# Eight batches of linear attention into a two-layer network: the third batch's first product as one plain product instead of seven

## The chip, the cores and the metric

The kernel runs on one core of a Trainium2 chip. The metric is the device time of one execution in microseconds. A core has TensorE (PE; its weight loads are listed as PEld), VectorE (DVE), ScalarE (ACT), GpSimd (POOL) and the queue of SyncE (SP), from which nearly all transfers are issued. Each engine works through its own instructions in the order in which they were written and waits by semaphores for the others, so a waiting instruction holds up everything behind it on its engine.

## The reference

There are 8 batches of 8 heads, 576 positions and 64 numbers per head. From q and k come feature vectors of 128 numbers, from those and v the attention output, and this output (4608 rows of 512) goes through two matrices with a leaky ReLU between them:

```python
r = np.maximum(x, 0.0); phi = np.concatenate([r * cos_w, r * sin_w], axis=-1)   # for q and k
kv  = np.einsum('bhsf,bhsd->bhfd', phi_k, v); z = np.sum(phi_k, axis=2)
out = np.einsum('bhsf,bhfd->bhsd', phi_q, kv) / (np.einsum('bhsf,bhf->bhs', phi_q, z)[..., None] + 1e-06)
x   = out.transpose(0, 2, 1, 3).reshape(4608, 512)
h   = x @ w_in                      # (4608, 512) @ (512, 2048)
y   = np.maximum(0.01 * h, h) @ w_out   # (4608, 2048) @ (2048, 512)
```

## The kernel before

The rows are cut into nine groups of 512: groups 0 to 7 are the first 512 positions of each batch, group 8 the last 64 positions of all eight. For each group the kernel makes the attention output (sum over k and v: `kv_sum`, L314; product with q and division: `num` and `divide`, L403 and L421, the result in the tile `xs`), turns it round so that features lie on partitions (tile `xT`), makes the first product (x by w_in) with the leaky ReLU into the tile `g`, and then the second product (`g` by w_out).

Both products exist in two forms. The plain form of the first product (`ffn1`, L475) takes 16 units for a group; a unit, called M, is four matmuls of 512 columns, and after every second unit ACT applies the leaky ReLU to 1024 columns. The form by seven (`ffn1s`, L619) is Strassen's: 4 parts of 7 products, each product a unit of four matmuls of 256 columns, 28 units in all. It needs sums of weight blocks (`w1_sum`, L579, eight operations once, kept in the tile `wext`), sums of blocks of xT (`x_sum`, L595, four for each group) and, for each of its parts, three copies, two additions and four leaky ReLUs of 512 columns (`ffn1e`, L649) on ACT and DVE. It works in four PSUM banks `ps_f`, which take the place of the two double banks `ps_h` of the plain form once that is no longer used. The second product by seven (`ffn2s`, L729) has 28 units too, called F here, F0 to F27, of four matmuls of 256 columns; it needs sums of `g` (`g_sum`, L681) and, once, of w_out (`weight_sum`, L540). Group 0 is plain in both products. `G7 = 1` and `F7 = 2` say from which group on the second and the first product go by seven: the first product is plain for groups 0 and 1.

The order of everything after the first groups is written out. Stretch g of the program interleaves the second product of group g with the first product of group g+1; a string for each stretch (`O`) gives the order of the units: F is a unit of the second product, M a plain one of the first, a digit a product of the seven, other letters the operations behind them. All other work has a place, a number on the same axis (16 places for each stretch; stretch 1 runs from 16 to 32), and `weave` (L915) puts it into the program in front of the unit that follows its place. A letter in the strings `e`, `We`, `Xe` names the engine for it: D is DVE, A ACT, P POOL. For batch b these are the loads (`L`), the feature maps of q (`q_prep`, two operations for each of four row blocks) and of k (`k_cos`, `k_sin`, nine each), the copies of v (`v_pairs`, two), the transposes of q's features by DMA, `kv_sum`, four `num`, and the transposition of `xs` to `xT`. The tiles for k's features (`kp`), for v (`vm`) and for `xs` exist once, so the next batch's may be written only after the last reader of the one before.

For groups 3 to 8 `xT` comes from a DMA transpose issued on SP. For group 2 it comes from TensorE (`x_transpose`, L382): for each of four row blocks four small transposes into the PSUM tile `ps_x` and a copy by ACT. That tile covers two banks; row blocks 0 and 1 lie in the first, 2 and 3 in the second. A write of TensorE into a bank waits for the copy out of that bank.

k, v and q arrive in four staging buffers (`stage`); some go to the tiles `ext` and `wext` instead, before these are needed for sums (`stage_tile`, L104).

Of the kernel before, what the change touches and what calls it, by code (L numbers as in the profile page):

```python
# [9 lines left out]
dt = mybir.dt  # L10
# [10 lines left out]
def kernel(  # L21
# [15 lines left out]
    B, H, S, D = q.shape  # L37
# [10 lines left out]
    NKC = DM // P  # L48
# [1 line left out]
    NG = B + 1  # L50
    NE = D + 2
    G7 = 1
    F7 = 2

    ctx.enter_context(tc.manual_schedule())

# [31 lines left out]
    def need(*keys):  # L88
        for key in keys:
            assert key in done, key  # L90
# [58 lines left out]
    w1 = {}  # L149
# [95 lines left out]
    kv = [const.tile([P, H, NE], dt.float16, name=f"kv{b}") for b in range(B)]  # L245
# [136 lines left out]
    def x_transpose(g, j, eng):  # L382

        need(("num", g, j))
        if j == 0:
            st["ps_x", g] = psum("h", [P, J, NKC, P], dt.float16, "ps_x")
        ps = st["ps_x", g][:, j]
        for c in range(NKC):
            nc.tensor.transpose(ps[:, c], st["xs", g][:, j, 2 * c : 2 * c + 2, :], ident)  # L389
        copy(eng, xT_tile(g)[:, j], ps)  # L390
        if j == J - 1:
            done.add(("xT", g))
# [430 lines left out]
    held = []  # L823
# [185 lines left out]
    for m in range(6):  # L1009
# [4 lines left out]
    units = []  # L1014

    TUNE = {'B': {2: {'L': None,
               'e': 'DDDDDPADAAAAPDPPPPPDDDAA',
               'kc': [14.1499, 14.4499, 14.3249, 14.3749, 13.9249, 14.4249, 13.8499, 14.2999, 14.2499],
               'ks': [14.3499, 14.0999, 14.0749, 14.2749, 14.1749, 14.2249, 14.1249, 13.7749, 14.3999],
               'mm': 16.0956,  # L1020
               'n': [16.4042, 17.139, 17.6138, 18.1982],
               'q': [10.357, 10.4856, 10.5499, 10.8713],
               'qT': [10.7428, 12.6999],
               'v': [13.3499, 10.9356],
               'x': [17.3129, 17.6764, 18.8869, 18.939],
               'xe': 'AAAA'},
           3: {'L': [10.6142, 13.1999, 13.4249, 18.1356],
               'e': 'AADADAAAPAPAAPAPDDAPADPA',
               'kc': [18.9042, 17.1651, 19.0521, 18.8347, 18.7042, 16.6173, 17.8347, 18.2295, 17.526],
               'ks': [19.3529, 17.4477, 17.4869, 19.226, 16.8173, 17.6451, 17.1912, 19.0129, 17.7077],  # L1030
               'mm': 20.4434,
               'n': [22.0086, 23.5738, 24.6173, 25.6608],
               'q': [16.4825, 17.1129, 13.6249, 17.0869],
               'qT': [18.1669, 18.9216],
               'v': [18.8695, 19.2651],
               'x': 27.0521},
           4: {'L': [16.7651, 24.7912, 19.1869, 19.1869],
               'e': 'APADPAPAPDADAAADAAAPDAPP',
               'kc': [34.7303, 36.2956, 33.1651, 35.9477, 35.7477, 34.6782, 35.8956, 35.2521, 32.4042],
               'ks': [34.6521, 35.1999, 29.6347, 32.3847, 35.0521, 32.6173, 32.4238, 34.7564, 33.1129],  # L1040
               'mm': 36.7912,
               'n': [38.5825, 40.0956, 43.5738, 42.0086],
               'q': [24.0956, 26.8782, 32.4434, 33.5129],
               'qT': [27.9216, 36.2434],
               'v': [27.226, 31.3999],
               'x': 44.0564},
           5: {'L': [33.4608, 28.7912, 37.6608, 37.6608],
               'e': 'APPADPDDAPDAPAAADAAPPDDP',
               'kc': [38.8782, 37.8086, 41.8347, 38.5303, 41.3129, 46.3564, 44.6564, 44.5782, 38.5564],
# [12 lines left out]
               'n': [67.9608, 69.0999, 70.8782, 72.2695],
               'q': [51.2521, 57.8347, 54.8782, 57.1234],
               'qT': [59.026, 60.4695],
               'v': [61.6869, 57.6608],
               'x': 72.8303},
           7: {'L': [59.426, 60.4173, 65.7956, 65.7956],
               'e': 'DPADADPAAPDPPPAAAPAAPADS',
               'kc': [81.4869, 81.1129, 72.4434, 76.2695, 69.1782, 75.179, 71.8956, 84.2695, 83.7477],
               'ks': [77.3129, 71.3999, 68.6173, 83.3738, 67.9216, 74.3564, 75.0521, 75.2103, 76.9651],  # L1070
               'mm': 85.6608,
               'n': [86.3564, 87.5738, 88.8173, 89.4869],
               'q': [71.9477, 72.7912, 73.4869, 83.426],
               'qT': [75.3999, 84.8173],
               'v': [74.1825, 76.4434],
               'x': 90.8782},
           8: {'L': [69.139, 83.5738, 87.6129, 87.8956],
               'e': 'ADAA',
               'kc': [],
               'ks': [],  # L1080
               'mm': 10.657,
               'n': [97.8086, 99.3999, 101.139, 102.9042],
               'q': [85.4608, 87.7477, 87.9477, 88.7651],
               'qT': [91.226, 100.2695],
               'v': [],
               'x': 103.1999}},
     'O': {1: 'MMMMMMMMMM',
           2: 'FFFFFFFFFFFFFFFFFFFFF15bsF63u27zy1a5ebc4d6Su2a3zeF17byF562s4uc3z7dFa1e5ySFb4c6ud327zFayecF4d',
           3: 'FFFF1FB5FFs613u2FzFaFF7yeBF5264scad3uFFzFe1bF7FFF5yFF6sc4u2F3zad7Fy1ebF456Fd2SFFuac7y3czeF4d',
           4: '1FF5b1s6u3FF2FazF7yFF45FebFs63udFzF7cy1eb2aFF625cSFu4Fa73yFzdFF1FF5Feb4F6s3u2zc7yFdeFcFFa4dF',  # L1090
           5: '1bF5s62a3uFF517zebySF62FFFFu4F3a57dc1zeysFbFFF4d6uF2aFFF375Fz1cFyebsFF62u3Fca47yFFzF4FdcFFed',
           6: '1b5Fs16uF372aFzebFFy5426FScF3UFzdeFa7F1y5bcF2asFFF6FF34FFduFz1e7yF5SFbc6uF47FdyF3z2ce4FFFaFd',
           7: '1Fb52s6u3z1F7aebFF2y5aFFF6uSF4F7F3zdcy1eF54b6u2aF7SFdF5c3yFz1FSeBcFFF4FdF6uF27y3cazeFF4FFFFd',
           8: '15FFb2s6auFF3z7y51Fe4b62s3UzFFa7FdF1ceFFFBy6F5c2SaF43FUzFF7Fdey1Fb4FF5F6FdsFuc3F7zeFy2F4aFcd',
           9: 'FFFFFFFFFFFFFFFFFFFFFFFFFFFF'},
# [17 lines left out]
     'We': ['PPDD', 'PDPP'],  # L1113
     'X': {2: [19.0912, 19.4156, 19.4469, 19.5738],
           3: [32.4825, 32.5021, 37.139, 34.7042],
           4: [47.0129, 48.6173, 51.1999, 49.3129],
           5: [59.9216, 62.2086, 65.4608, 62.5303],
           6: [76.6173, 78.3564, 82.0086, 76.7912],
           7: [92.5912, 92.7912, 99.226, 97.139],
           8: [103.2521, 109.3129, 112.7521, 108.9651]},  # L1120
     'Xe': {2: 'DPDD', 3: 'DPPD', 4: 'PDPD', 5: 'DPDD', 6: 'DDDP', 7: 'PPDD', 8: 'PDDD'},
     'held': 10.2928}

    for g in range(NG):
        order, seen = TUNE["O"][g + 1], {}
# [105 lines left out]
```

## Time and profile before

| what | value |
|---|---|
| median of three runs | 274.75 us (274.72 to 275.25) |
| the profiled execution | 275.64 us |
| its span, first to last instruction | 273.9 us |
| PE busy | 264.3 us, 97% of the span |
| DVE busy | 209.3 us, 76% |
| ACT busy | 189.5 us, 69% |
| POOL busy | 114.1 us, 42% |
| mean granted clock of TensorE | 0.998 |

A timeline row gives the start, the duration, the engine, the line, the operation, what it writes and reads, the shapes and the count; in brackets stands the idle time of the engine before it and what ended that. Rows for several instructions merge those that follow each other. The busy time of a matmul covers its way through the array, so its row (273 ns for 256 columns) is longer than the distance to the next one; distances are read from start to start.

### The profile page before, as it was taken

How to read it: one execution, taken by the hardware profiler on the slowest of the kernel's cores; microseconds unless marked ns; L12 is line 12 of the kernel's file. 1: busy time of each engine (PE TensorE's matmuls, PEld its weight loads, DVE VectorE, ACT ScalarE, POOL GpSimd, SP SyncE). 2: the span in 40 equal slices, each digit the busy share in tenths (PEclk: the TensorE clock that was granted, in tenths of full speed). 3: DMA queues.
4: the chain of work that ended last, by engine and by line, in shares of the span. 5: the costliest groups of instructions: out<-in, count | busy, mean ns of one | idle time of the engine just before them, and what ended most of it. 6: DMA issues, size and time to landing. Idle time of an engine off the chain costs nothing.

```text
span 273.9 us, 7194 instructions
## 1 busy us (share of the span) xinstructions
PE 264.3 (97%) x2925; PEld 223.2 (81%) x2925; DVE 209.3 (76%) x430; ACT 189.5 (69%) x344; POOL 114.1 (42%) x93
## 2 busy tenths in 40 slices
PE   8799999999889999999999999999999999999994
PEld 3576555556779999999999999989999899999983
DVE  4760595698887899889797979886987778867652
ACT  7766537589968998988797878967857365645500
POOL 2496006992738818996693477330003001000000
PEclk9999999999999999999999999999999999999999
DMA  6999999989999499879979975847199051200314
GB/s 228 369 392 410 383 398 373 357 203 254 300 217 364 117 207 272 237 248 191 253 255 213 306 226 174 181 118 149 45 123 224 2 115 42 77 14 29 112 43 115
DMA packets 75040, 57.08 MB, mean 208 GB/s; under 512 B 47232, under 2 KB 63616, under 8 KB 74624
## 3 DMA queue, kind: packets, MB, share of 16 engines
q1 hardware_dynamic: 74400, 56.11, 73.8%
q10 hardware_dynamic: 608, 0.52, 0.6%
q8 instruction: 23, 0.38, 0.6%
q14 instruction: 9, 0.07, 0.1%
HBM read 36.70 MB, written 9.44 MB: 168 GB/s over the span
## 4 chain that ended last, share of the span: by engine, by line
PE 88%; DMA 3%; ACT 3%; DVE 1%; POOL 1%; SPq 1%; issue 1%; ACTq 0%
PE ps L755 32%; PE ps_f L638 31%; PE ps_h L486 10%; PE ps_o L512 5%; PE ps_kv L326 4%; DMA kst<-in_k_dram 3%; PE ps_num L412 3%; ACT qp L251 1%; PE ps_f L755 1%; POOL kp L253 1%; PE ps_qt L398 1%; ACT xT L259 1%; PE ps_xth L464 1%; PE ps_x L389 0%; SPq L135 0%
## 5 line engine op out<-in xcount | busy, mean ns | idle before, releaser
L755 PEld LDWEIGHTS <-g 128*128 128x128 f16 x640 | 61.5, 98 | 7.0 <-ACT g L665 0.2
L755 PE MATMUL ps<-w,g 128*128 128x256 f16 x496 | 65.4, 273 | 0.0
L665 ACT ACTIVATE g<-ps_f 128x512 f16<-128x512 f32 x84 | 48.3, 596 | 17.4 <-DVE ps_f L538 10.7
L638 PEld LDWEIGHTS <-w 128*128 128x128 f16 x448 | 48.7, 114 | 1.8 <-DVE ext L538 0.6
L638 PE MATMUL ps_f<-xT,w 128*128 128x256 f16 x336 | 48.7, 273 | 0.5 <-DVE ext L538 0.3
L638 PEld LDWEIGHTS <-wext 128*128 128x128 f16 x336 | 36.3, 114 | 0.7
L755 PE MATMUL ps<-T,ext 128*128 128x256 f16 x240 | 31.9, 273 | 0.0
L486 PE MATMUL ps_h<-xT,w 128*128 128x512 f16 (+1 forms) x144 | 28.9, 355 | 0.1
L253 POOL TENSOR_SCALAR kp<-kst,cos_t 128x256 f16<-128x256 f32 (+1 forms) x20 | 26.8, 1346 | 4.9 <-DMA kst<-in_k_dram 3.6
L755 PEld LDWEIGHTS <-ext 128*128 128x128 f16 x256 | 24.6, 98 | 2.6
L638 PE MATMUL ps_f<-X,wext 128*128 128x256 f16 x176 | 26.5, 273 | 0.0
L253 POOL TENSOR_SCALAR kp<-kst,sin_t 128x256 f16<-128x256 f32 x16 | 21.4, 1346 | 11.7 <-ACT ext L774 6.4
L486 PEld LDWEIGHTS <-w 128*128 128x128 f16 x144 | 16.0, 114 | 10.8
L538 DVE TENSOR_TENSOR ps_f<-ps_f,u 128x512 f32<-128x512 f32 x28 | 19.4, 694 | 6.4 <-ACT u L259 4.2
L538 DVE TENSOR_TENSOR y<-ps_f,s 128x512 f32<-128x512 f32 x28 | 19.2, 686 | 4.6 <-PE ps_f L638 3.4
L538 DVE TENSOR_TENSOR osb<-ps,ext 128x512 f32<-128x512 f32 x23 | 15.8, 687 | 7.2 <-PE ps L755 7.1
L259 ACT COPY u<-ps_f 128x512 f32<-128x512 f32 x25 | 14.7, 587 | 8.9 <-PE ps_f L638 8.6
L428 DVE TENSOR_TENSOR xs<-ps_num,rden 128x512 f16<-128x512 f32 x28 | 19.4, 691 | 1.0
L496 ACT ACTIVATE g<-ps_h 128x1024 f16<-128x1024 f32 x16 | 15.8, 1023 | 6.1 <-PE ps_h L486 6.1
L665 ACT ACTIVATE g<-y 128x512 f16<-128x512 f32 x28 | 17.7, 632 | 3.1 <-DVE y L538 3.1
L755 PE MATMUL ps<-ext,g 128*128 128x256 f16 x128 | 18.1, 273 | 0.0
L259 ACT COPY ps_f<-ps_f 128x512 f32<-128x512 f32 x24 | 13.7, 573 | 5.2 <-PE ps_f L638 4.5
(117 smaller groups left out, 464.4 us busy)
## 6 DMA issues: line engine op xcount, KB each, us to landing
out_dram<-osb SPq DMA_DIRECT2D x32, 256.0 KB, 2.8
qst<-in_q_dram SPq DMA_DIRECT2D x7, 1024.0 KB, 9.4
kst<-in_k_dram SPq DMA_DIRECT2D x6, 1152.0 KB, 9.5
vst<-in_v_dram SPq DMA_DIRECT2D x5, 1152.0 KB, 7.5
w2st<-in_moe_w_out_dram SPq DMA_DIRECT2D x3, 1024.0 KB, 11.9
vst<-in_v_dram SPq DMA_DIRECT2D x4, 576.0 KB, 8.0
ext<-in_moe_w_in_dram SPq DMA_DIRECT2D x4, 512.0 KB, 9.6
kst<-in_k_dram SPq DMA_DIRECT2D x2, 576.0 KB, 8.5
```

Of the source, the lines that this page charges most:

```text
L253: eng.tensor_scalar(out=o, in0=i, scalar1=0.0, scalar2=col, op0=ALU.max, op1=ALU.mult)
L259: nc.scalar.copy(o, i)
L326: nc.tensor.matmul(ps[:, o, (c - lo) * NE : (c - lo + 1) * NE], lhsT=st["kp", b][sl, c, j, :], rhs=vm[sl, c, j, :], start=(j == 0), stop=( ...
L412: nc.tensor.matmul(ps[lo:hi, h // 4, (h % 4) * NE : (h % 4 + 1) * NE], lhsT=qpT[:, h, lo:hi], rhs=kv[b][:, h, :],)
L428: nc.vector.tensor_tensor(out=xs, in0=ps[:, :, 0 : 4 * NE].rearrange("p a (b e) -> p a b e", e=NE)[:, :, :, 0:D], in1=rden.rearrange("p (a ...
L486: nc.tensor.matmul(ps[:, m % 2, lo:hi], lhsT=w1[m // 4, c][0][:, w1[m // 4, c][1], m % 4 : 512 : 4], rhs=xT[:, lo // P : hi // P, c, :], s ...
L496: nc.scalar.activation(st["g", g][:, m - 1 : m + 1, :], ps, AF.Lrelu)
L512: nc.tensor.matmul(st["ps_o", g, tt], lhsT=st["g", g][:, m, tt * P : (tt + 1) * P], rhs=w2[:, m, :], start=(m == 0), stop=(m == NFT - 1),)
L538: eng.tensor_tensor(out=o, in0=a, in1=b, op=op)
L638: nc.tensor.matmul(ps[:, mi * HT : (mi + 1) * HT], lhsT=a[:, c, 2 * r0 + mi : 512 : 4], rhs=b[:, c], start=(n in (1, 5) and mi == 0 and c ...
L665: nc.scalar.activation(st["g", g][:, m : m + 2, r * HT : (r + 1) * HT], {"a": A, "c": y22, "e": E, "d": B_}[e].rearrange("p (m t) -> p m t ...
L755: nc.tensor.matmul(ps[:, tt], lhsT=a[:, i, tt * P : (tt + 1) * P], rhs=b[:, i], start=(first and i == 0), stop=(i == NPR - 1 and (apart or ...
```

## The change

`F7` becomes 3: the first product of group 2 is plain, 16 units M instead of 28 units by seven, and with it go group 2's four `x_sum` and its 36 operations of `ffn1e`; eight leaky ReLUs of 1024 columns take their place. In stretch 1 the order is now 24 units F, then the 16 M, then the last four F. The four PSUM banks `ps_f` are taken up one stretch later.

Group 2's `xT` still comes from TensorE, but its row blocks now alternate between the two banks of `ps_x`, and the places put row block 3 ahead of 2, with `kv_sum` of batch 3 behind them and ahead of the first M.

k of batch 3 is staged in `wext`; so the weight sums, which are kept there, must follow the feature maps of that batch. They move from places 10 to 23 to places 25 to 39, seven of the eight on DVE (before: three).

All places, engine letters and strings are new. In stretch 1 the feature maps of batch 2's k, before at place 14, now stand at places 16 to 17, and `kv_sum` of batch 2 comes after F6 (before: after F0).

```diff
-    F7 = 2
+    F7 = 3
...
-    in_wext = {("w1", 1), ("k", 1)}
+    in_wext = {("w1", 1), ("k", 1), ("k", 3)}
...
-            st["ps_x", g] = psum("h", [P, J, NKC, P], dt.float16, "ps_x")
-        ps = st["ps_x", g][:, j]
+            st["ps_x", g] = psum("h", [P, 2, J // 2, NKC, P], dt.float16, "ps_x")
+        ps = st["ps_x", g][:, j % 2, j // 2]
...
-        need(("kv", 1), *(("W", bp, i) for i in {1: (), 2: (1,), 4: (2,), 3: (1,)}[n]))
+        need(*(("kp", 3, j, f, 0) for j in range(T) for f in (0, D)), *(("W", bp, i) for i in {1: (), 2: (1,), 4: (2,), 3: (1,)}[n]))
...
     TUNE = {'B': {2: {'L': None,
-               'e': 'DDDDDPADAAAAPDPPPPPDDDAA',
-               'kc': [14.1499, 14.4499, 14.3249, 14.3749, 13.9249, 14.4249, 13.8499, 14.2999, 14.2499],
-               'ks': [14.3499, 14.0999, 14.0749, 14.2749, 14.1749, 14.2249, 14.1249, 13.7749, 14.3999],
-               'mm': 16.0956,
-               'n': [16.4042, 17.139, 17.6138, 18.1982],
-               'q': [10.357, 10.4856, 10.5499, 10.8713],
-               'v': [13.3499, 10.9356],
-               'x': [17.3129, 17.6764, 18.8869, 18.939],
+               'e': 'DDDPAAPPDPPPPDADDAPADPDD',
+               'kc': [16.2326, 16.5963, 16.189, 16.0799, 16.1454, 16.4654, 16.1017, 16.3199, 17.009],
+               'ks': [16.2108, 16.6617, 16.1672, 16.2981, 16.5308, 16.2763, 16.0581, 16.1235, 16.3417],
+               'mm': 18.3817,
+               'n': [19.1536, 20.5635, 21.6872, 22.6472],
+               'q': [10.6142, 10.7428, 14.307, 14.3713],
+               'v': [10.4856, 10.357],
+               'x': [21.3999, 21.7199, 24.509, 24.2544],
...
-           3: {'L': [10.6142, 13.1999, 13.4249, 18.1356],
-               'e': 'AADADAAAPAPAAPAPDDAPADPA',
-               'mm': 20.4434,
+           3: {'L': [10.8713, 14.1785, 14.2428, 19.2429],
+               'e': 'AAAAAPAPAPDAPPADDPDADPAP',
+               'mm': 24.6181,
...
-           2: 'FFFFFFFFFFFFFFFFFFFFF15bsF63u27zy1a5ebc4d6Su2a3zeF17byF562s4uc3z7dFa1e5ySFb4c6ud327zFayecF4d',
+           2: 'FFFFFFFFFFFFFFFFFFFFFFFFMMMMMMMMMMMMMMMMFFFF',
...
-     'T': [10.1642, 10.4213, 13.1249, 10.807],
-     'W': [[10.2285, 12.8499, 16.2695, 19.3842], [10.6785, 20.5912, 20.6434, 22.7042]],
-     'We': ['PPDD', 'PDPP'],
-     'X': {2: [19.0912, 19.4156, 19.4469, 19.5738],
+     'T': [10.2285, 14.8874, 14.1142, 15.3499],
+     'W': [[24.9817, 28.5963, 29.5503, 29.6693], [25.9363, 27.8908, 29.6098, 38.7042]],
+     'We': ['DDDP', 'DDDD'],
...
-     'held': 10.2928}
+     'held': 16.9272}
```

More of the change, by code (lines that the diff above doesn't have):

```diff
@@ L1077 @@
-           8: {'L': [69.139, 83.5738, 87.6129, 87.8956],
-               'e': 'ADAA',
+               'e': 'DDDPAAPPDPPPPDADDAPADPDD',
[4 more added lines that the diff above has]
+               'q': [10.6142, 10.7428, 14.307, 14.3713],
+               'qT': [14.6624, 16.2544],
@@ new lines @@
+               'v': [10.4856, 10.357],
+               'x': [21.3999, 21.7199, 24.509, 24.2544],
+               'xe': 'AAAA'},
+           3: {'L': [10.8713, 14.1785, 14.2428, 19.2429],
+               'e': 'AAAAAPAPAPDAPPADDPDADPAP',
+               'kc': [19.0346, 20.9272, 19.2131, 19.0644, 21.2363, 19.1239, 21.6544, 21.589, 21.3454],
+               'ks': [18.9751, 22.7781, 21.7854, 21.2908, 19.0049, 19.0941, 22.8435, 21.7526, 21.1817],
+               'mm': 24.6181,
+               'n': [25.2908, 26.0181, 27.1908, 27.7817],
+               'q': [19.1834, 19.4726, 17.6544, 21.6217],
+               'qT': [21.5563, 22.7126],
+               'v': [24.1454, 21.5235],
+               'x': 28.5308},
@@ new lines @@
+           4: {'L': [17.3726, 26.0999, 24.8726, 24.8726],
+               'e': 'APPAPAPPDDADPDDAPADADAAA',
+               'kc': [36.3086, 35.026, 34.0477, 35.0782, 29.7586, 35.1999, 33.9695, 34.3564, 35.3999],
+               'ks': [35.226, 34.7042, 33.8503, 36.2303, 35.2782, 29.7883, 36.2695, 35.9216, 35.1738],
+               'mm': 37.6608,
+               'n': [38.5303, 39.7477, 42.8521, 40.6434],
+               'q': [27.0272, 27.4726, 28.4654, 28.8726],
+               'qT': [29.2363, 29.3454],
+               'v': [28.6617, 29.6396],
+               'x': 43.3608},
@@ new lines @@
+           5: {'L': [33.7877, 29.7288, 34.0086, 34.0086],
+               'e': 'PDPDAAADPPAAAPPDAPAPPAAA',
+               'kc': [45.139, 49.5129, 42.3303, 39.9216, 40.2695, 43.0521, 39.5738, 44.2695, 42.6782],
+               'ks': [43.5738, 40.0956, 40.5912, 50.1564, 45.0999, 42.1825, 40.2303, 50.2086, 49.6608],
+               'mm': 51.426,
+               'n': [52.4956, 56.7912, 55.6129, 58.0347],
+               'q': [40.3086, 42.7303, 42.3825, 42.9042],
+               'qT': [43.3999, 51.9216],
+               'v': [45.1782, 43.439],
+               'x': 60.2434},
@@ new lines @@
+           6: {'L': [41.6608, 48.7912, 52.4695, 52.4695],
+               'e': 'PDPADAAPPDAPADPPDDPPADAA',
+               'kc': [60.4434, 57.9825, 53.3129, 54.3564, 55.5347, 60.5614, 56.0695, 57.4608, 60.6732],
+               'ks': [60.0956, 53.8816, 56.1216, 57.6608, 60.6061, 61.1651, 53.7877, 60.2956, 61.5129],
+               'mm': 61.8347,
+               'n': [65.8347, 67.9477, 71.0521, 73.8347],
+               'q': [52.4434, 53.8503, 59.1999, 59.2521],
+               'qT': [57.5129, 61.4608],
+               'v': [60.5838, 61.1129],
+               'x': 75.0129},
@@ new lines @@
+           7: {'L': [60.6508, 61.9695, 69.8347, 69.8347],
+               'e': 'APDPDPPPDAPPDADDAPPAAPPA',
+               'kc': [73.5129, 73.2869, 76.2173, 76.3216, 75.0912, 76.939, 76.9912, 76.2956, 71.1999],
+               'ks': [73.339, 78.39, 81.3129, 78.3005, 76.2434, 73.4608, 76.9651, 76.4695, 82.5564],
+               'mm': 83.026,
+               'n': [83.7738, 86.8782, 88.1216, 89.4869],
+               'q': [65.139, 68.7912, 67.8956, 74.5303],
+               'qT': [71.2521, 83.0782],
+               'v': [76.4173, 76.2695],
+               'x': 91.1999},
@@ L1079 @@
+           8: {'L': [76.9129, 78.3229, 78.4123, 83.7216],
+               'e': 'ADAP',
                'kc': [],
@@ L1081 @@
                'mm': 10.657,
-               'n': [97.8086, 99.3999, 101.139, 102.9042],
-               'q': [85.4608, 87.7477, 87.9477, 88.7651],
-               'qT': [91.226, 100.2695],
+               'n': [98.0086, 99.7477, 100.9651, 103.5738],
+               'q': [81.8608, 83.3999, 91.426, 92.2695],
+               'qT': [87.5477, 97.8608],
                'v': [],
-               'x': 103.1999}},
+               'x': 104.2956}},
      'O': {1: 'MMMMMMMMMM',
-           2: 'FFFFFFFFFFFFFFFFFFFFF15bsF63u27zy1a5ebc4d6Su2a3zeF17byF562s4uc3z7dFa1e5ySFb4c6ud327zFayecF4d',
@@ new lines @@
+           6: '15FFb62s1Ua3Fz57eb6yFF4s2uF37FczFaey5FdsF1F4b6duF13zF7Fecb2FayFFFF5F6FFFU7ScF2aFy4cF3z4FdFed',
+           7: '15FFbsF2a6U1537zFFFyFeb4Fc6sUF3FdF7F2zaFy1FeF5bcs246F3Fad5u71FzFeysc4BF6U23dFzF7ycFeFaF4FdFF',
+           8: '1b5SF62Fu1a75FFyF3Fczse4bF3F6FFdFu2a7FFz5eyF14FFb62cdaFsFUF753yzcF1FF4eFBSd6uF3zF7FyF2e4caFd',
+           9: 'FFFFFFFFFFFFFFFFFFFFFFFFFFFF'},
[17 rows of a table added]
+     'We': ['DDDP', 'DDDD'],
+     'X': {3: [30.0181, 31.109, 33.819, 33.8816],
+           4: [44.7912, 48.4434, 52.3912, 49.4608],
+           5: [62.0477, 64.9651, 65.6869, 62.3564],
+           6: [78.3452, 78.3676, 82.3303, 81.8086],
+           7: [94.8521, 97.2869, 98.7042, 98.3564],
+           8: [107.5738, 111.0521, 113.6608, 110.1825]},
@@ L1124 @@
+     'Xe': {3: 'DPDD', 4: 'PDDD', 5: 'DPDP', 6: 'PPPD', 7: 'PDDP', 8: 'PDPP'},
+     'held': 16.9272}
     for g in range(NG):
```

64 lines of the change are left out of this document (3 added, 61 removed), and 30 rows, old and new, of the table TUNE.

## The prediction

> **What bounds the kernel now.** I read the page first, engines and slices.
>
> ```profile
> span 273.9 us, 7194 instructions
> ...
> PE 264.3 (97%) x2925; PEld 223.2 (81%) x2925; DVE 209.3 (76%) x430; ACT 189.5 (69%) x344; POOL 114.1 (42%) x93
> PE   8799999999889999999999999999999999999994
> PEclk9999999999999999999999999999999999999999
> ...
> L755 PE MATMUL ps<-w,g 128*128 128x256 f16 x496 | 65.4, 273 | 0.0
> ```
>
> TensorE sets the time at full granted clock, and outside the first slices and the last it falls below nine tenths only in slices 11 and 12, about 68 to 82 us. So an edit counts by the TensorE time that it adds and by the idle time that it removes there. Then PE's timeline in order of time; these rows bound stretch 1 and show its holes.
>
> ```profile
> 53.46 12.25 PE L486 MATMUL ps_h<-xT,w 128*128 128x512 f16 x56
> 65.55 0.60 PE L755 MATMUL ps<-w,g 128*128 128x256 f16 x4
> ...
> 73.66 0.38 PE L389 MATMUL ps_x<-ident,xs 128*128 128x128 f16 x4 [1.24 <-ACT xT L259]
> ...
> 78.25 0.38 PE L389 MATMUL ps_x<-ident,xs 128*128 128x128 f16 x4 [0.67 <-ACT xT L259]
> ...
> 80.73 0.63 PE L638 MATMUL ps_f<-xT,w 128*128 128x256 f16 x4 [0.35 <-DVE ext L538]
> ...
> 98.80 2.01 PE L755 MATMUL ps<-w,g 128*128 128x256 f16 x16
> ```
>
> Stretch 1 runs from 65.7 (the first F) to 98.8 (four F in a row open stretch 2). Twice row blocks of `xT` wait for the copy out of the bank they share, and the first product waits for what `xT` feeds. Prices of units come from the chain of waits.
>
> ```profile
> 53.62 12.09 PE ps_h L486 x56
> 75.61 1.75 PE ps L755 x16
> 128.57 1.75 PE ps_f L638 x16
> 107.79 1.25 PE ps_kv L326 x72
> 75.36 0.25 PE ps_num L412 x8
> 77.36 0.24 PE ps_x L389 x4
> ```
>
> Per matmul 12.09/56 = 0.216 us for 512 columns and 1.75/16 = 0.109 for 256, in either product. So M costs 0.864, F or one of the seven 0.437, one `kv_sum` 1.25, one `num` 0.25, one row block 0.23.
>
> **The sum on TensorE.** Removed: 28 units by seven, 12.24 us. Added: 16 M, 13.82. Net **+1.58 us**. Work in stretch 1 before: 28 F 12.24, first product 12.24, two `kv_sum` 2.5, eight `num` 2.0, four row blocks 0.9, together 29.9; from 65.7 that ends at 95.6. It ended at 98.8, so 3.2 us were lost: at the three holes the idle 1.24 + 0.67 + 0.35 and three times the array running empty and full (0.273 - 0.109), 2.75, and some 0.45 in small gaps. With the change the work ends at 65.7 + 31.45 = 97.15. The question is what waits remain. For that I walk the queues of ACT, DVE and POOL by these rows.
>
> ```profile
> 50.71 5.07 POOL L253 TENSOR_SCALAR kp<-kst,sin_t 128x256 f16<-128x256 f32 x4
> 55.77 2.48 POOL L253 TENSOR_SCALAR kp<-kst,cos_t 128x256 f16<-128x256 f32 x1
> 60.82 2.69 POOL L253 TENSOR_SCALAR kp<-kst,cos_t 128x256 f16<-128x256 f32 x1
> 72.36 2.25 POOL L253 TENSOR_SCALAR kp<-kst,cos_t 128x256 f16<-128x256 f32 x2
> 74.57 1.14 POOL L261 CAST vm<-vst 128x1152 f16<-128x1152 f32 x1
> 58.12 1.16 ACT L259 CAST vm<-vst 128x1152 f16<-128x1152 f32 x1
> 63.45 2.10 ACT L251 ACTIVATE kp<-kst,cos_t 128x256 f16<-128x256 f32 x5
> 65.45 1.92 ACT L496 ACTIVATE g<-ps_h 128x1024 f16<-128x1024 f32 x2
> 67.44 0.60 ACT L333 CAST kv<-ps_kv 128x528 f16<-128x528 f32 x1
> 70.20 0.71 ACT L251 ACTIVATE qp<-qst,cos_t 128x512 f16<-128x512 f32 x1
> ...
> 71.43 0.70 ACT L251 ACTIVATE qp<-qst,cos_t 128x512 f16<-128x512 f32 x1
> 78.67 0.58 ACT L259 COPY xT<-ps_x 128x512 f16<-128x512 f16 x1 [0.47 <-PE ps_x L389]
> 67.40 0.42 DVE L538 TENSOR_TENSOR ext<-g 128x512 f16<-128x512 f16 x1 [0.33 <-ACT g L496]
> 65.33 0.34 DVE L253 TENSOR_SCALAR kp<-kst,sin_t 128x256 f16<-128x256 f32 x1
> 65.59 0.34 DVE L253 TENSOR_SCALAR kp<-kst,cos_t 128x256 f16<-128x256 f32 x1
> 76.08 0.69 DVE L428 TENSOR_TENSOR xs<-ps_num,rden 128x512 f16<-128x512 f32 x1
> L538 DVE TENSOR_TENSOR ps_f<-ps_f,u 128x512 f32<-128x512 f32 x28 | 19.4, 694 | 6.4 <-ACT u L259 4.2 <-PE ps_f L638 2.1
> L538 DVE TENSOR_TENSOR wext<-w,wext 128x1024 f16<-128x1024 f16 x1 | 0.7, 684 | 0.0
> ```
>
> In a queue ACT thus gives 0.42 for a k operation, 1.23 for a q block (70.20 to 71.43), about 0.5 for a copy; DVE 0.27 for a k operation; POOL 1.13 to 1.27, but about 2.6 where DVE is packed (55.8 to 63.5).
>
> *`kv_sum` of batch 2.* It now stands after seven F: TensorE is there at 65.7 + 3.06 = 68.8. On ACT nothing but the leaky ReLUs precedes the five k operations: the last leaky ReLU, at 66.4 to 67.4 before because k operations stood ahead of it, should run at 65.9 to 66.9, and the five end at 69.0. On DVE the last two sums over `g` wait for that leaky ReLU (67.8), then come five k operations: 69.2. POOL has eight; from about 51 on (the first row above is its start on this batch's k, and its q block takes the time of the weight sums it had until then) it needs 8 x 1.27 = 10 to 8 x 2.6 = 21 us, so 61 to 72; DVE has a pause from about 60.5 to 63.5 in its new order (a sum over `g` waits for a leaky ReLU), so I take 66. DVE ends last: wait **0.45** (0 if it is early, 3 by POOL's worst). Everything behind it on TensorE moves with it.
>
> *`num` and the row blocks of batch 2.* ACT still has a q block ahead of the copy of `kv_sum`: 0.15 at the first `num`. From then on two to four F stand between two `num`, 0.9 to 1.75 us, against 1.4 to 1.5 from a `num` to the end of its division (75.36 to 76.77); no hole. Row blocks 0 and 1 go to different banks, 3 and 2 come six F later, when the copies are long done: the two bank waits are gone. The copy of block 2 ends about 1.0 us after its transposes (78.25 to 79.25) and is hidden by `kv_sum` of batch 3, 1.25; without that cover the first M would wait 0.8.
>
> *`kv_sum` of batch 3* is what is late next. TensorE reaches it at 80.0. `kp` exists once, so all 18 k operations of batch 3 follow `kv_sum` of batch 2, that is 70.5. ACT, from 69.0, has before it: a copy 0.5, four q blocks 4.9, a copy of `kv` 0.6, six k operations 2.5, two copies of `xT` 1.1 with 0.25 of waiting, a v copy 1.1: 80.0. POOL has seven k operations and a v copy: 70.5 + 7 x 1.18 + 1.14 = 79.9, needed half-way through, at 80.6. All three arrive together: **0.2** (0 to 4, the third case below).
>
> *The sixteen M.* 53.62 to 65.71 shows 56 such matmuls without a hole. ACT has 8.2 us of leaky ReLU and 4.7 of q and v of batch 4 in 15 us; by its order a v copy, a q block and a v copy (1.1 + 1.2 + 1.1) stand among the last three leaky ReLUs and push the last from 1.2 to some 2.5 after M15; F1 of stretch 2, its first reader, comes five F = 2.2 after: **0.3**.
>
> *The rest of the change.* Weight sums move to DVE (7 x 0.69 = 4.8 us) beside the M, where DVE no longer has group 2's eight additions (5.5) and `x_sum`: nothing, as long as DVE has them done before the first by-seven unit of stretch 2, some 15 us on. Stores held from group 0 move behind two transposes on SP; their data lies in buffers no one waits for before stretch 1's first result. k of batch 3 goes to `wext`, whose last reader before is batch 1's k work ahead of stretch 1. I cost these at nothing.
>
> Stretch 1 then ends at 97.15 + 0.45 + 0.15 + 0.2 + 0.3 + 0.2 of small gaps (half as many as before, since half the stretch is M) = 98.45, against 98.8: **0.35 us less**. From there to the end the work is the same and the new order has no less room:
>
> ```profile
> 98.80:126.00 27.20, 27.20 (x387) 25.33 (x386) 25.33 (x54) 24.57 (x51) 22.04 (x16) 1.00 1.01 244
> 182.09 0.60 PE L638 MATMUL ps_f<-xT,wext 128*128 128x256 f16 x4
> 182.83 1.06 PE L638 MATMUL ps_f<-xT,w 128*128 128x256 f16 x8
> ```
>
> In the table by stretches (length, then busy time of PE, PEld, DVE, ACT, POOL) TensorE is never idle in 98.8 to 126, and after that I found one hole, 0.3 at 182.8. Little is left to gain there. The profiled execution took 275.64, 1.74 over its span, and 0.9 above the median of 274.75; I take the difference to the median: 274.75 - 0.35 = **274.4 us**.
>
> **The rivals.** *Everything arrives early.* If none of my waits shows, 1.15 us more are gained: 273.2. For it: ACT loses 36 small operations in exchange for eight. Against: three queues end within 0.3 us of TensorE by the walk.
>
> *POOL decides stretch 1 (slower).* If its operations on batch 3's k cost 1.83, the mean of the seven in 50.71 to 63.51, `vm` is ready at 70.5 + 12.8 + 1.1 = 84.4 and `kv_sum` waits 3.8 instead of 0.2: 278.0. It turns my gain into over 0.2% of loss from a mean of 1.5 on. For it: the rows of 2.48 and 2.69. Against: 1.13 in 72.36, where DVE had divisions and few k operations as it will again. The Trainium skill, SBUF — State Buffer, "Who interferes with whom", says that a VectorE instruction in a 2-port mode, or with two SBUF inputs against a reading GpSimd one, shares a port pair with GpSimd and that the second to start "fully blocks". The 2.6 us beside packed DVE and the 1.13 beside divisions from PSUM fit it; by that rule the weight sums, now on DVE, would also slow POOL's q of batch 4, which has some 10 us of room.
>
> *A late load.* k of batch 6 is issued at place 48.79 and first used by ACT at place 53.31; 14 units, a `kv_sum` and a `num` stand between, 7.6 us, and SP may run ahead by about 1.5, no further than the last store of the stretch before.
>
> ```profile
> kst<-in_k_dram SPq DMA_DIRECT2D x1, 1152.0 KB, 7.2
> kst<-in_k_dram SPq DMA_DIRECT2D x1, 1152.0 KB, 9.5
> ```
>
> These loads landed 7.2 to 9.5 after issue, so ACT would stand 0 to 1.9 us with the copies for the by-seven parts behind it. With the other new places that stands for holes in stretches 2 to 7: 0.9 to 1.9 more, 275.3 to 276.3. Against: that the program before has hardly one.
>
> **How the numbers follow.** No change is what lies within 0.2%, 0.55 us, about what a measurement of this kernel can tell. My forecast holds 0.48 (273.9 to 275.2: faster 0.12, same 0.34, slower 0.02), everything early 0.22 (faster), POOL 0.12 (slower), late loads and new holes 0.18 (slower 0.16, same 0.02). That gives faster 0.34, same 0.36, slower 0.30. The likeliest case lies on the line between two, so the range goes from 273.2, the first rival, to 276.4, the dearer end of the third; beyond is POOL's case and half of what is left.
>
> **What would show it.** Right: no row of `ps_x` with a bank wait; 64 matmuls of 512 columns in stretch 1 at 0.216; a wait of under 0.6 at each `kv_sum` there, ended by DVE at the first and by ACT or POOL at the second; stretch 2 beginning near 98.4. Wrong: a wait over 1 us at `kv_sum` of batch 3 ended by POOL; M with holes, which would mean that ACT's q and v hold the double bank; or holes over 0.5 us after 100, above all behind ACT near 135.

## The result and the profile after

The changed kernel takes 274.46 us (median of 15 runs, 273.68 to 275.55) against 275.06 us for the kernel before on the same chip (15 runs, 274.72 to 275.94). The ratio is 0.9979 with a 95% interval of 0.9969 to 0.9988: 0.6 us, or 0.2%, faster. The forecast was 274.4 us and 0.35 us less than before. Its sum held; where it placed the waits did not, as the sections below show.

The page of the changed kernel, engines and slices:

```profile
span 272.6 us, 7060 instructions
...
PE 264.4 (97%) x2877; PEld 218.4 (80%) x2877; DVE 205.4 (75%) x419; ACT 179.5 (66%) x311; POOL 128.9 (47%) x104
...
PE   7899999999999999999999999999999999999993
PEclk9999999999999999999999999999999999999998
```

TensorE is busy as long as before in all (264.4 us), but in stretch 1 alone 32.20 us against 30.99; ahead of it its busy time is 0.9 less. The dents of slices 11 and 12 are gone, and ACT has 10 us less work, POOL 15 more. PE's timeline of stretch 1 shows what is left of holes:

```profile
52.38 12.25 PE L486 MATMUL ps_h<-xT,w 128*128 128x512 f16 x56
64.47 0.93 PE L755 MATMUL ps<-w,g 128*128 128x256 f16 x7
65.75 2.47 PE L755 MATMUL ps<-w,g 128*128 128x256 f16 x21 [0.35 <-ACT g L496]
68.15 1.32 PE L326 MATMUL ps_kv<-vm,kp 64*128 64x66 f16 x72
...
74.07 0.42 PE L412 MATMUL ps_num<-kv,qpT 128*128 128x66 f16 x8
74.47 0.38 PE L389 MATMUL ps_x<-ident,xs 128*128 128x128 f16 x4
...
78.23 0.60 PE L755 MATMUL ps<-ext,g 128*128 128x256 f16 x4
79.07 0.38 PE L389 MATMUL ps_x<-ident,xs 128*128 128x128 f16 x4 [0.24 <-ACT xT L259]
79.38 1.32 PE L326 MATMUL ps_kv<-vm,kp 64*128 64x66 f16 x72
80.64 1.92 PE L486 MATMUL ps_h<-xT,w 128*128 128x512 f16 x8
...
89.46 6.21 PE L486 MATMUL ps_h<-xT,w 128*128 128x512 f16 x28
95.51 2.78 PE L755 MATMUL ps<-w,g 128*128 128x256 f16 x24
```

The row at 95.51 holds the last four F of stretch 1 (16 matmuls, 1.75 us) and the first two of stretch 2, so stretch 2 begins at 97.26. Stretch 1 lasts from 64.47 to 97.26, 32.79 us, against 65.55 to 98.80, 33.25 us, before: 0.46 less. Taking off the 31.45 us of work, 1.34 us are lost. Worked out from start to start (what passes beyond 0.109 for each matmul of 256 columns, 0.25 for a `num`) they lie here: F1's last matmul 0.51 (64.47 + 7 x 0.109 = 65.23, but it starts at 65.75); row block 1 0.15; row block 2, which comes after block 3, 0.40 (78.23 + 0.437 = 78.67, but 79.07); the rest, some 0.3 in all, in pieces of about 0.1 or less.

What these waits wait for stands in ACT's timeline of the changed kernel:

```profile
64.67 1.02 ACT L496 ACTIVATE g<-ps_h 128x1024 f16<-128x1024 f32 x1 [0.70 <-PE ps_h L486]
...
73.84 0.59 ACT L259 COPY xT<-ps_x 128x512 f16<-128x512 f16 x1
...
77.24 1.14 ACT L259 CAST vm<-vst 128x1152 f16<-128x1152 f32 x1
78.43 0.59 ACT L259 COPY xT<-ps_x 128x512 f16<-128x512 f16 x1
```

The last leaky ReLU of group 1 ends at 65.69, and F1 goes on at 65.75. The copy of row block 0 ends at 74.43, and block 1 starts at 74.47. The copy of block 3 ends at 79.02, and block 2 starts at 79.07. So both row blocks start right behind the copy of the block before them, although that one lies in the other bank. `kv_sum` of batch 2, at 68.15, starts right behind DVE's last k operations of that batch, which end at 68.10:

```profile
67.23 0.87 DVE L253 TENSOR_SCALAR kp<-kst,sin_t 128x256 f16<-128x256 f32 x3
```

### The profile page after: what moved, and what is told of

Read it like the earlier page. It is cut to its first block, busy times and chain, and to the rows that moved or that the text cites. A ratio compares the mean times of both kernels' runs of the same rounds, so it can differ in the third digit from the quotient of the medians.

```text
span 272.6 us, 7060 instructions
## 1 busy us (share of the span) xinstructions
PE 264.4 (97%) x2877; PEld 218.4 (80%) x2877; DVE 205.4 (75%) x419; ACT 179.5 (66%) x311; POOL 128.9 (47%) x104
## 4 chain that ended last, share of the span: by engine, by line
PE 89%; DMA 3%; DVE 3%; POOL 1%; issue 1%; SPq 1%; ACT 1%; DVEq 0%
PE ps L755 33%; PE ps_f L638 26%; PE ps_h L486 15%; PE ps_o L512 5%; PE ps_kv L326 4%; DMA kst<-in_k_dram 3%; PE ps_num L412 3%; PE ps_f L755 1%; POOL kp L253 1%; PE ps_qt L398 1%; PE ps_xth L464 1%; PE ps_x L389 0%; DVE u L261 0%; ACT g L496 0%; SPq L135 0%
## 5 line engine op out<-in xcount | busy, mean ns | idle before, releaser
L665 ACT ACTIVATE g<-ps_f 128x512 f16<-128x512 f32 x72 | 42.0, 599 | 19.9 <-PE ps_f L638 10.2
L486 PE MATMUL ps_h<-xT,w 128*128 128x512 f16 (+1 forms) x208 | 43.5, 363 | 0.1
L638 PE MATMUL ps_f<-xT,w 128*128 128x256 f16 x288 | 42.1, 273 | 0.2 <-DVE u L261 0.2
L496 ACT ACTIVATE g<-ps_h 128x1024 f16<-128x1024 f32 x24 | 24.2, 1025 | 13.1 <-PE ps_h L486 13.1
L638 PEld LDWEIGHTS <-wext 128*128 128x128 f16 x288 | 31.2, 114 | 0.5
L253 POOL TENSOR_SCALAR qp<-qst,cos_t 128x512 f16<-128x512 f32 (+1 forms) x10 | 19.5, 1947 | 9.2 <-DMA qst<-in_q_dram 7.7
L638 PE MATMUL ps_f<-X,wext 128*128 128x256 f16 x144 | 21.5, 273 | 0.0
L253 POOL TENSOR_SCALAR qp<-qst,sin_t 128x512 f16<-128x512 f32 (+1 forms) x10 | 19.6, 1963 | 0.0
L538 DVE TENSOR_TENSOR ext<-g 128x512 f16<-128x512 f16 (+1 forms) x24 | 14.1, 589 | 4.7 <-ACT g L496 3.0
L538 DVE TENSOR_TENSOR y<-ps_f,s 128x512 f32<-128x512 f32 x24 | 16.4, 685 | 1.4 <-PE ps_f L638 1.3
```

Source lines behind the costliest of these rows:

```text
L253: eng.tensor_scalar(out=o, in0=i, scalar1=0.0, scalar2=col, op0=ALU.max, op1=ALU.mult)
L486: nc.tensor.matmul(ps[:, m % 2, lo:hi], lhsT=w1[m // 4, c][0][:, w1[m // 4, c][1], m % 4 : 512 : 4], rhs=xT[:, lo // P : hi // P, c, :], s ...
L496: nc.scalar.activation(st["g", g][:, m - 1 : m + 1, :], ps, AF.Lrelu)
L538: eng.tensor_tensor(out=o, in0=a, in1=b, op=op)
L638: nc.tensor.matmul(ps[:, mi * HT : (mi + 1) * HT], lhsT=a[:, c, 2 * r0 + mi : 512 : 4], rhs=b[:, c], start=(n in (1, 5) and mi == 0 and c ...
L665: nc.scalar.activation(st["g", g][:, m : m + 2, r * HT : (r + 1) * HT], {"a": A, "c": y22, "e": E, "d": B_}[e].rearrange("p (m t) -> p m t ...
```

## The experiments

All times are medians; the kernel before stood at 275.05 to 275.07 us beside each set of runs.

**The banks undone.** The changed kernel with the layout of `ps_x` of before:

```diff
-            st["ps_x", g] = psum("h", [P, 2, J // 2, NKC, P], dt.float16, "ps_x")
-        ps = st["ps_x", g][:, j % 2, j // 2]
+            st["ps_x", g] = psum("h", [P, J, NKC, P], dt.float16, "ps_x")
+        ps = st["ps_x", g][:, j]
```

> The changed kernel with the alternation of the two banks undone and nothing else; row blocks keep the order 0, 1, 3, 2. Prediction's theory: the alternation took the bank waits away, so with neighbours in one bank again block 1 waits for the copy of block 0 and block 2 for that of block 3, 0.5 to 1.3 us more, 275.0 to 275.7. Rival: a write of one block waits for the copy of the block before it whatever the bank, as the rows at 74.47 and 79.07 of the changed kernel suggest (each starts 0.05 after that copy ends), and only the distance between the blocks in the program counts; then nothing changes: the same rows and 274.5 within 0.3.

Measured: 274.46 us (274.13 to 275.12), ratio to before 0.9979 (0.997 to 0.9989), as the changed kernel itself. Its PE timeline has the same rows, 0.15 us after the time of the changed kernel:

```profile
74.23 0.42 PE L412 MATMUL ps_num<-kv,qpT 128*128 128x66 f16 x8
74.63 0.38 PE L389 MATMUL ps_x<-ident,xs 128*128 128x128 f16 x4
...
78.38 0.60 PE L755 MATMUL ps<-ext,g 128*128 128x256 f16 x4
79.22 0.38 PE L389 MATMUL ps_x<-ident,xs 128*128 128x128 f16 x4 [0.24 <-ACT xT L259]
```

The same 0.15 and 0.40 are lost. Alternating the banks does nothing here: the program makes a row block wait for ACT's copy of the block before it, in whichever bank of the one tile it lies, as the wait was the same for neighbours in one bank and in two. (The description of the kernel above, which has the wait go by the bank, is wrong there.) What made the waits of 1.24 and 0.67 short is where blocks and copies stand. In the kernel before, ACT's copy of block 0 began 2.14 us after the block's transposes, behind k and q operations in ACT's queue; in the changed kernel it began 0.43 after (73.41 to 73.84). Block 3 followed block 2 at once; now one F stands between the last two blocks. The kernel before, first PE's timeline, then ACT's:

```profile
70.91 0.39 PE L389 MATMUL ps_x<-ident,xs 128*128 128x128 f16 x4
```

```profile
73.05 0.56 ACT L259 COPY xT<-ps_x 128x512 f16<-128x512 f16 x1
```

**Row block 3 earlier.** The changed kernel with block 3 before one more F, so that its copy is over when block 2 comes:

```diff
-               'x': [21.3999, 21.7199, 24.509, 24.2544],
+               'x': [21.3999, 21.7199, 24.509, 23.9],
```

> The changed kernel with row block 3 one unit F earlier, so that two F instead of one stand between it and block 2. If block 2 waits for the copy of block 3 (0.40 us lost at 79.07), the wait goes and the whole is 0.3 to 0.45 us faster, about 274.05. If that wait comes from elsewhere (the division of block 3, or the copies' turn on ACT), it stays or moves to block 3 and the time is 274.5.

Measured: 275.21 us (274.36 to 276.04), ratio 1.0005 (0.9992 to 1.0018). Block 2's wait is gone, and yet the kernel is 0.75 us slower than the changed one. Both expectations missed. First ACT's timeline, then PE's:

```profile
79.17 0.59 ACT L259 COPY xT<-ps_x 128x512 f16<-128x512 f16 x1 [0.75 <-PE ps_x L389]
79.66 1.16 ACT L259 CAST vm<-vst 128x1152 f16<-128x1152 f32 x1
```

```profile
80.86 1.32 PE L326 MATMUL ps_kv<-vm,kp 64*128 64x66 f16 x72 [0.63 <-ACT vm L259]
```

Block 3's copy has moved ahead of the copy of v on ACT too. ACT stands 0.75 us for the transposes, the copy of v ends late, and `kv_sum` of batch 3 waits (0.79 lost). A wait of 0.40 on TensorE was exchanged for one of 0.79 behind another queue. In the profiles that makes stretch 1 longer by 0.39 us (33.18 against 32.79); what the rest of the 0.75 is stays open.

**F1 and F2 exchanged.** The changed kernel; F2 needs only the part of `g` that is there early:

```diff
     def f2h(g, i):
+        if g == 1 and i in (1, 2):
+            i = 3 - i
         return lambda: ffn2s(g, i // 2, (i % 2,))
```

> The changed kernel with F1 and F2 of stretch 1 exchanged, so that the first reader of the last leaky ReLU of group 1 comes one F later. The wait of F1 (0.35 idle, 0.51 lost) then shrinks to under 0.1. Theory one: TensorE then reaches the kv sum of batch 2 at 67.7, before VectorE's last feature map of k at 68.1, and waits there 0.3 to 0.45, as predicted: 274.4 in all. Theory two: the kv sum had 0.4 us of room and the gain stays: 274.0.

Measured: 274.43 us (273.73 to 275.56), ratio 0.998 (0.9967 to 0.9993), no difference to the changed kernel. PE's timeline:

```profile
65.93 3.31 PE L755 MATMUL ps<-w,g 128*128 128x256 f16 x28
69.34 1.39 PE L326 MATMUL ps_kv<-vm,kp 64*128 64x66 f16 x72
```

The seven F now run without a hole (28 x 0.109 = 3.05 us, to 68.98), and `kv_sum` of batch 2 waits 0.35 for the feature maps of k. The wait that I had put there existed; it was hidden behind F1's.

**The old kernel with row block 2 earlier.** The worth of a hole by itself, measured in the kernel before:

```diff
-               'x': [17.3129, 17.6764, 18.8869, 18.939],
+               'x': [17.3129, 17.6764, 18.5, 18.939],
```

> The kernel before with row block 2 two units F earlier, nothing else. Block 3 then need not wait for the copy of block 2 (0.84 us lost at 77.2 to 78.25). If TensorE's holes in stretch 1 are worth what they last, the kernel before gains 0.6 to 0.85: 274.3 against 275.06. If what follows (copy, sum of blocks, addition on VectorE) ends last at the first product anyway, the hole at 80.73 grows by what was gained: 275.0.

Measured: 274.29 us (274.03 to 274.52), ratio 0.9967 (0.9955 to 0.9979), 0.76 us less. The second hole (0.84 lost: 0.67 idle and the array running empty and full) is gone, the others stay. This hole was worth about what it lasts, and one number of the old kernel gives as much as the whole change.

**The plain product alone.** The kernel before with `F7 = 3`, the new order of units (with the last seven F at the end), no `x_sum` of group 2, and all places of stretch 1 kept where they were relative to the units, but for the sums of `g` for group 2 and the last two weight sums, which have the changed kernel's places:

```diff
-    F7 = 2
+    F7 = 3
...
-           2: 'FFFFFFFFFFFFFFFFFFFFF15bsF63u27zy1a5ebc4d6Su2a3zeF17byF562s4uc3z7dFa1e5ySFb4c6ud327zFayecF4d',
+           2: 'FFFFFFFFFFFFFFFFFFFFFMMMMMMMMMMMMMMMMFFFFFFF',
```

> One part of the change alone on the kernel before: F7 = 3, group 2's first product as 16 plain units behind the 21st F of stretch 1, its sums of blocks dropped, the order and the engines of all else in stretch 1 as before (the last two weight sums, which write the weights that the plain form reads, and group 2's sums over g go to the places of the changed kernel). Theory: TensorE gets 1.58 us more work and the two holes between row blocks (1.40 + 0.84) stay, the third becomes the wait for the last copy, 0.5 to 0.8: 1.4 to 1.9 us slower than before, 276.4 to 277.0. Rival: the plain form pays by itself, since ScalarE and VectorE lose 36 small operations: not slower than 275.06.

Measured: 277.91 us (277.59 to 279.49), ratio 1.0109 (1.0078 to 1.0141), 2.84 us more. Two holes of before stay (1.26 and 0.84 lost here), the third is gone, and stretch 1 lasts 34.09 us (64.49 to 98.58), 0.84 more than before, about what the sum says (1.58 - 0.51 for the third hole - 0.2 for small gaps). A new hole stands in stretch 2, first in PE's timeline, then in DVE's:

```profile
96.83 1.91 PE L755 MATMUL ps<-w,g 128*128 128x256 f16 x16
100.73 1.91 PE L755 MATMUL ps<-w,g 128*128 128x256 f16 x16 [1.99 <-DVE osb L538]
```

```profile
97.24 0.42 DVE L538 TENSOR_TENSOR ext<-ext,g 128x512 f16<-128x512 f16 x1
97.58 0.95 DVE L538 TENSOR_TENSOR g<-g 128x1536 f16<-128x1536 f16 x1
98.45 0.69 DVE L538 TENSOR_TENSOR ext<-ext,g 128x1024 f16<-128x1024 f16 x1
99.06 0.69 DVE L538 TENSOR_TENSOR w<-w,w 128x1024 f16<-128x1024 f16 x1
99.66 0.42 DVE L538 TENSOR_TENSOR ext<-ext,g 128x512 f16<-128x512 f16 x1
99.99 0.68 DVE L538 TENSOR_TENSOR osb<-ps,ext 128x512 f32<-128x512 f32 x1
```

The first F of stretch 2 need the PSUM banks that the last outputs of stretch 1 (`osb`) leave, and these additions stand behind six sums of `g` and of weights on DVE (the first at 96.78), some of which wait for the last leaky ReLUs.

**The plain product with four F last.** The same kernel, the order of the units as in the changed kernel:

```diff
-           2: 'FFFFFFFFFFFFFFFFFFFFFMMMMMMMMMMMMMMMMFFFFFFF',
+           2: 'FFFFFFFFFFFFFFFFFFFFFFFFMMMMMMMMMMMMMMMMFFFF',
```

> The kernel before with the plain first product of group 2 as in the run that did this part alone, but with four F behind the sixteen M as in the changed kernel, where that run had seven. Theory one (the plain product itself costs stretch 1 some 0.8 us, and the 2.15 us at the start of stretch 2 came from the order of the last F, whose sums on DVE stood behind the last leaky ReLU): the hole at the start of stretch 2 goes or falls under 0.5, the time is 275.1 + 0.8 + 0 to 0.5 = 275.9 to 276.4. Theory two (DVE's other work there, behind the same leaky ReLU, makes the hole whatever the order of F): it stays at 1.5 to 2.5, 277.4 to 278.4.

Measured: 275.53 us (275.26 to 276.46), ratio 1.0016 (1.0004 to 1.0028). The new hole is gone (the first theory, whose estimate was 0.4 too high):

```profile
72.62 0.38 PE L389 MATMUL ps_x<-ident,xs 128*128 128x128 f16 x4 [1.09 <-ACT xT L259]
...
77.21 0.38 PE L389 MATMUL ps_x<-ident,xs 128*128 128x128 f16 x4 [0.67 <-ACT xT L259]
...
96.69 3.66 PE L755 MATMUL ps<-w,g 128*128 128x256 f16 x32
```

So three F fewer behind the M were worth 2.4 us, and the plain product in the old places makes the kernel 0.45 us slower. It is not a gain in itself.

**The cover taken away.** The changed kernel with `kv_sum` of batch 3 ahead of row block 2 instead of behind it:

```diff
-               'mm': 24.6181,
+               'mm': 24.45,
```

> The changed kernel with the kv sum of batch 3 ahead of row block 2 instead of behind it. The prediction's price: without that cover the first M waits 0.8 for the last copy. Block 2's own wait of 0.40 goes, since the kv sum now stands between it and block 3: net 0.3 to 0.5 slower, 274.85. If the copy of the last block is not what the first M needs, 0.4 faster, 274.05.

Measured: 275.03 us (274.5 to 275.4), ratio 0.9995 (0.998 to 1.001), 0.57 more than the changed kernel. PE's timeline:

```profile
79.87 0.40 PE L389 MATMUL ps_x<-ident,xs 128*128 128x128 f16 x4
81.12 1.89 PE L486 MATMUL ps_h<-xT,w 128*128 128x512 f16 x8 [0.85 <-ACT xT L259]
```

Without its cover the copy of block 2 costs the first M 1.03 us (81.12 - 79.87 - 0.22), less the 0.40 that block 2 itself no longer waits.

**New places in the changed kernel.** All three holes at once: F1 and F2 exchanged, feature maps of k on DVE before stretch 1, a copy of v from ACT to DVE, one sum of w_out earlier (`T`), row blocks 1 and 3 moved:

```diff
...
-               'x': [21.3999, 21.7199, 24.509, 24.2544],
+               'x': [21.3999, 21.9, 24.509, 23.9],
...
-               'e': 'AAAAAPAPAPDAPPADDPDADPAP',
+               'e': 'AAAAAPAPAPDAPPADDPDADPDP',
...
-     'T': [10.2285, 14.8874, 14.1142, 15.3499],
+     'T': [10.2285, 14.6, 14.1142, 15.3499],
```

> The changed kernel with the waits of stretch 1 taken out one by one: F1 and F2 exchanged; VectorE's five k operations of batch 2 ahead of the last leaky ReLU's sums, and one weight sum moved into VectorE's pause, so that the kv sum of batch 2 does not wait in turn; v of batch 3, first half, on VectorE right behind that kv sum instead of late on ScalarE; row block 1 one F later and block 3 one F earlier. Lost before: 0.51 + 0.15 + 0.40. If these holes are the whole loss of stretch 1: 0.8 to 1.05 faster than the changed kernel, 273.5. If each is replaced by the next queue that comes late (VectorE's divisions, GpSimd's nine microseconds on k of batch 3): 274.1 to 274.5.

Measured: 274.34 us (273.74 to 275.32), ratio 0.9972 (0.9955 to 0.9989), 0.1 us less than the changed kernel. The three holes are gone, but DVE has become late for a `num` (0.68 lost):

```profile
72.74 0.43 PE L412 MATMUL ps_num<-kv,qpT 128*128 128x66 f16 x8 [0.52 <-DVE xs L428]
```

**Two places in the old kernel.** The kernel before, row block 2 earlier as above, row block 1 a few units later, behind its copy:

```diff
-               'x': [17.3129, 17.6764, 18.8869, 18.939],
+               'x': [17.3129, 17.95, 18.5, 18.939],
```

> The kernel before with row block 2 two F earlier, as in the run before, and row block 1 two F later, so that it stands behind the copy of block 0. Of the 1.26 us lost there 0.4 to 0.5 should stay, and up to 0.2 come at block 3: 0.5 to 0.8 faster than with block 2 alone, 273.6. If the copies' place in ScalarE's queue ends last in any order, nothing: 274.3.

Measured: **273.31 us** (273.06 to 274.01), ratio 0.9933 (0.9908 to 0.9957), 1.76 us less than before by the medians; the interval reaches from 1.2 to 2.5 us. In the profiles stretch 1 is 1.21 us shorter (32.04, from 64.37 to 96.41, against 33.25), and what the rest is stays in part open. It beats both kernels, with the first product by seven. Block 1 still loses 0.39 of 1.40 us, and the first unit by seven now waits longer (0.88 lost, 0.51 before):

```profile
72.61 0.38 PE L389 MATMUL ps_x<-ident,xs 128*128 128x128 f16 x4 [0.22 <-ACT xT L259]
...
77.02 0.60 PE L755 MATMUL ps<-ext,g 128*128 128x256 f16 x4
78.34 0.63 PE L638 MATMUL ps_f<-xT,w 128*128 128x256 f16 x4 [0.71 <-ACT vm L259]
```

**The plain product and the two places.** The kernel with four F last and these two places together:

```diff
-               'x': [17.3129, 17.6764, 18.8869, 18.939],
+               'x': [17.3129, 17.95, 18.5, 18.939],
```

> The run with the plain product and four F last, and besides row block 1 of xT at 17.95 and row block 2 at 18.5, the places that alone made the kernel before 1.8 us faster. Theory one (the two parts are independent: what the places give is what their holes last, with either form of the product): the holes of 1.26 and 0.84 go but for 0.4, so 1.7 less than the run without them. Theory two (what is removed there is lost at the first M or at kv_sum of batch 3, whose queues on ACT are as full as in the changed kernel): under 1.0 less.

Measured: 274.03 us (273.87 to 274.79), ratio 0.9957 (0.994 to 0.9973), 1.5 us less than without the places; the parts add up, nearly. Against the kernel with the same places and the product by seven it is 0.72 slower by the medians of four and six runs. In the two profiles stretch 1 differs by 0.18 only (65.73 to 97.95, 32.22, against 32.04). So of the 1.58 us that the plain product adds most is won back: 0.88 for the hole at the first unit by seven, which does not exist here, and some 0.5 in smaller gaps. That 0.72 + 0.88 also comes near 1.58 is chance.

## Why the prediction was right, and where not

**The sum on TensorE (+1.58) held.** The 28 matmuls from 89.46 to 95.51 take 0.216 us each, as estimated, and the 24 of 256 columns from 95.51 to 98.13 take 0.109.

**The start was misread by 0.15.** The walk begins stretch 1 at 65.7, where a row of M ends, but the first F starts at 65.55. The stretch thus took 33.25 us before and lost 3.35 of them, not 3.2. The length forecast for it after the change, 98.45 - 65.7 = 32.75, was met (32.79); that it became 0.46 shorter and not 0.35 is this misreading.

**The total of the waits held, 1.34 us measured against 1.3, but by misses that offset each other, which is luck:**

- *`kv_sum` of batch 2, 0.45.* It waited 0.1 at most (65.75 + 21 x 0.109 = 68.04 to 68.15). The wait was there (0.35 with F1 and F2 exchanged), but F1 had already waited 0.51 for the last leaky ReLU. That step was missing. I had moved `kv_sum` behind F6 in the walk, and counted only what that does to `kv_sum`; before, its 1.25 us stood between F0 and F1 and covered the leaky ReLU. POOL's eight k operations, for which I took an end at 66, ended at 63.2 (60.98 + 2.25 in the rows of POOL below).
- *The first `num`, 0.15.* It did not wait.
- *"The two bank waits are gone."* This step failed. The wait goes by the tile and not by the bank, as the kernel with the banks undone shows. Blocks 1 and 2 lost 0.15 and 0.40 instead of 1.40 and 0.84, by their distance in the program alone.
- *`kv_sum` of batch 3 as cover of block 2's copy, price 0.8.* Right: 1.03 without it.
- *`kv_sum` of batch 3, 0.2.* It waited 0.08 at most (79.07 + 0.23 to 79.38). ACT's copy of v ended at 78.38 and POOL's at 78.86, where I had 80.0 and 79.9, with TensorE there at 80. From the start of the stretch that is 13.9 and 14.4 us, against 14.3 and 14.2 in the walk. The queues were as near as I thought; block 2's unforeseen wait gave them the rest. The earlier row block 3, which took that wait away, made `kv_sum` lose 0.79.
- *The sixteen M without a hole*: right. *F1 of stretch 2, 0.3*: no wait; 24 F matmuls run through from 95.51 to 98.13, 0.109 each.

**The rest of the change at nothing.** Nearly: from the start of stretch 2 to the end of the span it takes 175.34 us against 175.10, with one hole, 0.37 lost ahead of the matmul at 173.43, where before had 0.30 at 182.8:

```profile
172.62 0.60 PE L755 MATMUL ps<-T,ext 128*128 128x256 f16 x4
173.43 0.60 PE L638 MATMUL ps_f<-xT,w 128*128 128x256 f16 x4 [0.20 <-DVE u L261]
```

By these two profiles the kernel should be 0.22 faster (0.46 - 0.24), by the medians it is 0.60. Two things in the other runs' traces narrow the gap. The hole near 173 stands in four of the six profiles of the changed kernel and its variants; in the other two (the banks undone, F1 and F2 exchanged) it is absent, and from stretch 2 to the end they take 174.99 and 175.08 us, no more than before. And the profile of before began stretch 1 late, by some 1.1 us (the last section says why), so that `kv_sum` of batch 2 found its features ready and took 1.25 us (66.08 to 67.33). In four profiles of variants that are the old kernel up to there and began early it stood inside `kv_sum`; the one with row block 2 earlier, first F at 64.56:

```profile
65.15 1.59 PE L326 MATMUL ps_kv<-vm,kp 64*128 64x66 f16 x72
66.67 1.05 PE L755 MATMUL ps<-w,g 128*128 128x256 f16 x8
```

It takes 1.52 there, and 1.46 to 1.52 in the four (1.39 in the one such variant that began late), while row block 1 loses 1.26 instead of 1.40 where its place is as before. So an early execution of the old kernel should take some 0.1 to 0.2 us longer in stretch 1 than its profile shows. With both the estimate for the change is 0.3 to 0.65 us, and the 0.60 lies in it. This is worked out from single profiles; no run isolates it.

**The rivals.** *Everything early* (273.2): no, 1.34 us are still lost in stretch 1. *POOL decides*: no. Its seven k operations of batch 3 took 8.0 us, 1.14 each, and not the 1.5 from which it would have counted. POOL's timeline of the changed kernel, with the end of batch 2's k ahead of it:

```profile
60.98 2.25 POOL L253 TENSOR_SCALAR kp<-kst,cos_t 128x256 f16<-128x256 f32 x2
69.72 2.34 POOL L253 TENSOR_SCALAR kp<-wext,sin_t 128x256 f16<-128x256 f32 x2 [6.48 <-PE ps_kv L326]
72.05 3.48 POOL L253 TENSOR_SCALAR kp<-wext,cos_t 128x256 f16<-128x256 f32 x3
...
77.72 1.14 POOL L261 CAST vm<-vst 128x1152 f16<-128x1152 f32 x1
```

DVE had divisions, reading PSUM, in that time. *A late load*: no hole near 135, where the load of k of batch 6 would have shown.

**Where the gain came from.** The change pays 1.58 us for the plain product, loses 0.51 at F1, and gets back 0.51 for the hole at the first unit by seven, 1.7 (1.40 + 0.84 - 0.15 - 0.40) for the distances between row blocks and copies, and some 0.3 in small gaps (0.6 before, 0.3 after). Most of the 1.7 is to be had without the plain product: the two places alone gave 1.76 by the medians, 1.21 in stretch 1 by the profiles, in the kernel before.

## What to carry to other kernels

When a step is moved, ask what it covered at its old place, and not only what it waits for at its new one. Of a hole behind a copy, ask first in which order the copy stands in its engine's queue and how far the next user is away in the program; two numbers in that order gave 1.8 us here by the medians, three times what the change of the algorithm with all its places gave. And test a gain of a rewrite against the old kernel with only its places mended.

## What the runs showed of the hardware

The start of stretch 1 differs between executions of programs that are alike up to there: the changed kernel began it at 64.47, the one with F1 and F2 exchanged, whose first difference comes after that point, at 65.93. Over the twelve profiles its first F came at 64.3 to 65.9 us, in two groups: 64.3 to 64.6 (eight of them) and 65.5 to 65.9 (four), in old and changed kernels alike. The profile of before fell in the late group and that of after in the early one, so 1.1 us of the difference between their spans (273.9 and 272.6) have nothing to do with the change.

The two groups part at the first loads. ACT's timeline of the kernel before, then that of the changed kernel:

```profile
10.83 1.24 ACT L259 CAST vm<-vst 128x576 f16<-128x576 f32 x2 [1.35 <-DMA vst<-in_v_dram]
```

```profile
9.72 1.25 ACT L259 CAST vm<-vst 128x576 f16<-128x576 f32 x2 [0.28 <-DMA vst<-in_v_dram]
```

In the eight early profiles ACT stands 0.2 to 0.5 us for this load of v, in the four late ones 1.35 to 1.8, and DVE's wait for the first load of k goes the same way (0.4 to 0.7 against 1.6 to 2.0). What makes these loads land later in some executions, the traces do not show. Distances within a stretch are nearly free of it (0.1 to 0.2 us in stretch 1 of the old kernel, as estimated above), and medians over many runs average over it; the spans of two single profiles are not free of it.
